# Attention and mixture of experts on one core: seven products from the fourth expert unit on, beside the last attention heads

## The chip, the cores and the metric

One core of a Trainium2 chip runs the whole program. The metric is the device time of one execution in microseconds (us); the times below are those of three runs, and the profile is one more execution with the hardware profiler on. PE is TensorE, DVE VectorE, ACT ScalarE, POOL GpSimd, SP SyncE, whose queue issues nearly all DMAs.

## The reference, cut to what matters

```python
# q, k, v: (2, 8, 768, 64); proj: (64, 6)
q_bucket, k_bucket = 6 sign bits of q @ proj and of k @ proj, as a number
scores = where(q_bucket == k_bucket, q @ k.T / 8, -1e9)
attn = softmax(scores); attn_out = attn @ v
x = attn_out as (2 * 768, 512)
# probs: (1536, 4), rows made to sum to 1; w1: (4, 512, 1024); w2: (4, 1024, 512)
for e in range(4):
    h = maximum(x @ w1[e], 0)
    out += p[:, e:e+1] * (h @ w2[e])
```

Everything is float32.

## The kernel before, in words

**Heads.** There are two batches of 8 heads, counted here as heads 0 to 15; heads 8 to 15 are batch 1. A head has 6 tiles of 128 rows of scores. `stage_s` ("S") makes a tile by 4 matmuls into the tile `sps` (two of them, taken in turn) from a head's four stacks `q1`, `al`, `ah`, `k2`, and a DVE instruction (line 432) takes the tile out and its row minimum. One step later ACT takes the exponential (448), two steps later DVE turns blocks (512, tile `t1`); after three tiles these go through DRAM (`scr`, `pt`). `stage_v` ("V") multiplies by `v` seven steps after the head's end, in 24 matmul records, and `stage_u` copies the result `pv` into `xraw`. `prep_head` makes the next head's stacks while a head runs: ACT writes `ah`; POOL copies it into `q1` (twice) and `k2`; DVE writes `al`; POOL copies `al` into `ah`; PE makes the hash `hps`; ACT writes its signs into `k2`; POOL turns them into bits in `al` and copies these into `k2`. The stacks have two buffers each, so a head's stacks are made while the head before still reads its own.

**Units.** A batch of the expert layer is 8 units (4 experts in two halves), 16 in all, counted 0 to 15. A unit has a first layer (x @ w1 into `hh` and `hl`, high and low halves of the ReLU) and a second layer (six tiles of 128 rows, each 12 matmuls of 512 columns into one PSUM bank `mps`, which DVE then adds to `acc`, line 754). All factors are split into a high and a low half, and a product is three matmuls. Units 0 to 5 (`unit`) make the first layer by 96 matmuls of 384 columns. Units 6 to 15 (`unit_fast`, from `FAST` on) make it by seven products of sums of blocks in place of eight, with 84 matmuls; their factors are sums of blocks of x (t1 to t4, by `x_ops_first` for batch 0, `x_ops_early` and `x_ops_late` for batch 1) and of w1 (s1 to s4, by `split_w1_fast` in the second layer of the unit before). In a sum, `combine` or `mix` is the DVE subtraction, then ACT writes the high half and POOL or DVE the low one. `mt` tiles hold the sums of products.

**Order.** Each engine runs its instructions in the order in which the program writes them. Attention of batch 1 is a generator, `attention()`, whose yields are costs; after each piece of an expert unit the main loop draws as much attention as a fixed pace allows:

```python
        while da < dm * ATT_PACE * n_att / n_moe:
            x = next(att, None)
```

Before, the attention is drawn to its end (`drained`) ahead of unit 5's second layer, and `x_ops_first` and the first call of `split_w1_fast` run in unit 5, when all scores have been made.

**PSUM.** Of eight banks, `ps2` holds two tiles of two banks each (`sps` during attention, `pa` and `pd` of a fast unit after it), and `ps1` four tiles of one bank (`mps`, `pv`, `hps`).

Of the kernel before, what the change touches and what calls it, by code (L numbers as in the profile page):

```python
# [48 lines left out]
FAST = 6  # L49
# [3 lines left out]
def tile_lsh_attention__then__domain_moe(  # L53
# [366 lines left out]
    def stage_s(b, h, t):  # L420
# [9 lines left out]
        pt = pp.tile([P, S], F32, tag="p", name="p")  # L430
# [179 lines left out]
    def attention():  # L610
# [3 lines left out]
        def do(op, i):  # L614
# [57 lines left out]
            elif op == "P":  # L672
                if i < n:
                    b, h, t = seq[i]
                    c = next(prep[0], None) if t >= PREP_AT else None
                    x = hseq.index((b, h))
                    if t == NT - 1 and x + 2 < len(hseq) and in_blocks(*hseq[x + 2]):
# [3 lines left out]
                    if t == NT - 1 and x + 1 < len(hseq):  # L681
                        load_v(*hseq[x + 1])
# [81 lines left out]
    def second_layer(b, u, first_u, hs, w2, xo=None):  # L764
# [6 lines left out]
        for s in range(NS - 1, -1, -1) if blocks else range(NS):  # L771
            for t in range(TS):
# [419 lines left out]
```

## Time and profile before

| what | value |
|---|---|
| median of three runs | 710.18 us (709.97 to 710.18) |
| the profiled execution: its own time | 710.34 us |
| its span, first to last instruction | 708.6 us |
| PE, DVE, ACT, POOL busy | 99%, 69%, 47%, 45% of the span |

The profiled execution is 0.16 us above the median, and 1.7 us of its time lie around the span. A matmul's record overlaps the next one's, so the rate of PE is read from starts, not from durations. In rows of groups, "mean ns" is the mean duration of one instruction; in a timeline the first number is the start and the second the duration, both in us from the span's start, and of a row "x2" the duration is that of both together.

### The profile page before, as it was taken

How to read it: one execution, taken by the hardware profiler on the slowest of the kernel's cores; microseconds unless marked ns; L12 is line 12 of the kernel's file. 1: busy time of each engine (PE TensorE's matmuls, PEld its weight loads, DVE VectorE, ACT ScalarE, POOL GpSimd, SP SyncE). 2: the span in 40 equal slices, each digit the busy share in tenths (PEclk: the TensorE clock that was granted, in tenths of full speed). 3: DMA queues.
4: the chain of work that ended last, by engine and by line, in shares of the span. 5: the costliest groups of instructions: out<-in, count | busy, mean ns of one | idle time of the engine just before them, and what ended most of it. 6: DMA issues, size and time to landing. Idle time of an engine off the chain costs nothing.

```text
span 708.6 us, 10175 instructions
## 1 busy us (share of the span) xinstructions
PE 700.9 (99%) x3726; PEld 593.9 (84%) x3726; DVE 490.2 (69%) x782; ACT 333.6 (47%) x655; POOL 316.5 (45%) x290
## 2 busy tenths in 40 slices
PE   8999999999999999999999999999999999999997
PEld 6766675878887978978888989899898989989896
DVE  6898888865585754755228797886857667685762
ACT  6887788543453544524234444343433434353340
POOL 6359578523352453503238555543514234341420
PEclk9999999999999999999999999999999999999999
DMA  6323354768997977867931121421212121122202
GB/s 150 68 47 75 75 116 84 216 170 204 264 247 225 238 182 223 238 214 231 237 105 60 61 89 54 153 63 60 93 57 90 46 75 59 61 90 59 90 1 89
DMA packets 90848, 87.76 MB, mean 124 GB/s; under 512 B 53168, under 2 KB 55728, under 8 KB 90800
## 3 DMA queue, kind: packets, MB, share of 16 engines
q1 hardware_dynamic: 89776, 86.80, 44.2%
q8 instruction: 29, 0.48, 0.3%
q10 hardware_dynamic: 1024, 0.33, 0.2%
q14 instruction: 19, 0.16, 0.1%
HBM read 65.04 MB, written 22.07 MB: 123 GB/s over the span
## 4 chain that ended last, share of the span: by engine, by line
PE 93%; DVE 2%; POOL 2%; issue 1%; ACT 1%; DMA 0%; POOLq 0%; DVEq 0%
PE mps L760 12%; PE mps L762 12%; PE mps L761 12%; PE pv L547 8%; PE mps L808 5%; PE mps L810 5%; PE mps L809 5%; PE sps L427 4%; PE sps L425 4%; PE ptps L493 4%; PE mps L1051 3%; PE mps L1050 3%; PE mps L1047 3%; PE pa L1050 2%; PE pa L1051 2%; PE pd L1051 2%
## 5 line engine op out<-in xcount | busy, mean ns | idle before, releaser
L760 PE MATMUL mps<-w2hi,hh 128*128 128x512 f32 (+1 forms) x388 | 151.0, 389 | 0.0
L761 PE MATMUL mps<-w2lo,hh 128*128 128x512 f32 (+1 forms) x388 | 150.5, 388 | 0.0
L762 PE MATMUL mps<-w2hi,hl 128*128 128x512 f32 (+1 forms) x388 | 150.4, 388 | 0.0
L1033 POOL TENSOR_TENSOR w2lo<-ws,w2hi 128x512 fp32r<-128x512 f32 x40 | 50.7, 1287 | 124.0 <-ACT w2hi L1032 121.1
L432 DVE TENSOR_SCALAR_CACHE_REDUCE p<-sps 128x768 f32<-128x768 f32 x96 | 90.0, 939 | 17.8 <-PE sps L427 16.3
L754 DVE SCALAR_TENSOR_TENSOR acc<-mps,pe,acc 128x512 f32<-128x512 f32 (+1 forms) x85 | 62.9, 740 | 56.0 <-PE mps L762 55.7
L448 ACT ACTIVATE p<-p,nb 128x768 f32<-128x768 f32 x96 | 89.5, 933 | 23.4 <-DVE p L432 23.0
L762 PEld LDWEIGHTS mps<-w2hi,hl 128*128 128x128 f32 x388 | 72.9, 188 | 15.7
L760 PEld LDWEIGHTS mps<-w2hi,hh 128*128 128x128 f32 x388 | 72.8, 188 | 15.0 <-issue 1.2
L761 PEld LDWEIGHTS mps<-w2lo,hh 128*128 128x128 f32 x388 | 72.9, 188 | 14.0
L547 PE MATMUL pv<-pt,tv 128*64 128x384 f32 x288 | 67.1, 492 | 0.0
L992 POOL TENSOR_TENSOR w1lo<-ws,w1hi 128x512 fp32r<-128x512 f32 x30 | 47.5, 1589 | 41.9 <-ACT w1hi L988 41.7
L808 PE MATMUL mps<-xs,w1hi 128*128 128x384 f32 x192 | 65.1, 339 | 0.0
L810 PE MATMUL mps<-xs,w1lo 128*128 128x384 f32 x192 | 64.5, 336 | 0.0
L809 PE MATMUL mps<-xs,w1hi 128*128 128x384 f32 x192 | 64.5, 336 | 0.0
L843 ACT ACTIVATE hh<-mps 128x384 fp32r<-128x384 f32 x48 | 23.4, 489 | 84.6 <-PE mps L810 84.6
L1060 ACT ACTIVATE hh<-mt 128x384 fp32r<-128x384 f32 x60 | 31.5, 525 | 58.4 <-DVE mt L1105 38.0
L844 DVE SCALAR_TENSOR_TENSOR hl<-mps,hh 128x384 fp32r<-128x384 f32 x48 | 26.4, 554 | 46.0 <-ACT hh L843 45.7
L425 PE MATMUL sps<-ah,q 128*128 128x384 f32 x192 | 53.5, 359 | 0.4 <-DVE p L432 0.4
L547 PEld LDWEIGHTS pv<-pt,tv 128*64 128x64 f32 x288 | 24.9, 136 | 32.2 <-issue 30.7
L512 DVE STREAM_TRANSPOSE t<-p 128x768 f32<-128x768 f32 x48 | 46.3, 965 | 7.7 <-ACT p L448 7.6
L242 POOL TENSOR_SCALAR q<-ah 64x768 fp32r<-64x768 f32 (+1 forms) x33 | 27.1, 821 | 54.5 <-ACT ah L354 40.1
(160 smaller groups left out, 1528.6 us busy)
## 6 DMA issues: line engine op xcount, KB each, us to landing
ws<-in_moe_w_dram SPq DMA_DIRECT2D x64, 512.0 KB, 3.9
scr<-t SPq DMA_DIRECT2D x16, 1152.0 KB, 7.5
pt<-scr SPq DMA_DIRECT2D x64, 288.0 KB, 5.7
tv<-in_v_dram SPq DMA_DIRECT2D x16, 192.0 KB, 4.5
tqk<-in_q_dram SPq DMA_DIRECT2D x30, 96.0 KB, 3.3
out_dram<-acc SPq DMA_DIRECT2D x11, 256.0 KB, 2.0
tqk<-in_k_dram SPq DMA_DIRECT2D x28, 96.0 KB, 3.1
rdb<-row SPq DMA_DIRECT2D x14, 192.0 KB, 6.4
```

The lines of the kernel that those rows point to most:

```text
L425: nc.tensor.matmul(ps[:, i, :NH], q1[:, sl], k1[:, i * NH : (i + 1) * NH], start=True, stop=False)
L432: nc.vector.tensor_scalar(out=two(pt), in0=ps[:, :, :NH], scalar1=MASKED, scalar2=MASKED, op0=ALU.min, op1=ALU.min, accum_out=nb,)
L448: nc.scalar.activation(pt, pt, ACTF.Exp, bias=nb, scale=-1.0, accum_out=dens[b, h, r][:, o : o + 1])
L547: nc.tensor.matmul(dst, vvs[b, h][:, c], pts[b, h, g][c], start=c == 0, stop=c == NT - 1, tile_position=(0, g * D),)
L754: nc.vector.scalar_tensor_tensor(out=acc, in0=ps, scalar=pcol, in1=acc, op0=ALU.mult, op1=ALU.add)
L760: nc.tensor.matmul(ps, hh[:, ts], w2hi[:, f, cs], start=n == 0, stop=False)
L761: nc.tensor.matmul(ps, hh[:, ts], w2lo[:, f, cs], start=False, stop=False)
L762: nc.tensor.matmul(ps, hl[:, ts], w2hi[:, f, cs], start=False, stop=n == FC - 1)
L808: nc.tensor.matmul(ps[:, :SB], w1hi[:, kk, fs], xhi[b, kk][:, sl], start=kk == 0, stop=False)
L809: nc.tensor.matmul(ps[:, :SB], w1hi[:, kk, fs], xlo[b, kk][:, sl], start=False, stop=False)
L810: nc.tensor.matmul(ps[:, :SB], w1lo[:, kk, fs], xhi[b, kk][:, sl], start=False, stop=kk == KD - 1)
L1033: nc.gpsimd.tensor_tensor(out=lo[:, c + o], in0=t[:, o], in1=hi[:, c + o].bitcast(F32), op=ALU.subtract)
```

## The change

`FAST` goes from 6 to 4, so units 4 and 5 use seven products too, while attention still runs beside unit 4. To make room:

- the sums of x for batch 0 are made in unit 3's first layer (t2, t3, t4) and at the start of its second layer (t1's halves, written over halves that unit 3 no longer reads);
- sums of both kinds and the products' `mt` tiles share a tag of their own, `pm`, with two buffers; the score tiles `p` of batch 1 have four in place of six, those of batch 0 alternate between both tags;
- a batch 0 fast unit keeps `pa` and `pd` in one-bank tiles, so that all its sums share `ps1` with `pv` and `hps`; its sums are made in place in the `mt` tiles, and it yields after each product;
- the stacks have one buffer per tag, in two sets for heads 0 to 13 by turns; heads 14 and 15 (`ALONE`) use the same set, so head 15's preparation is written after head 14's last tile of scores, followed by a yield of `ALONE_GAP`;
- `v` of a head is loaded in its own second step, from two buffers, in place of the last step of the head before, from three;
- the operands of batch 1 are spread over other tiles, six of seven in units 5 and 6.

```diff
-FAST = 6
+FAST = 4
+ALONE = 14
+ALONE_GAP = 2100
+EARLY = 5
...
+    def p_tile(b):
+        p_turn[0] += 1
+        if b == 0 and p_turn[0] % PP_BUFS >= PP_BUFS - 2:
+            return pair_tile([P, S], "p")
+        return pp.tile([P, S], F32, tag="p", name="p")
+
+    def pair_tile(shape, name):
+        return pp.tile(shape, F32, tag="pm", name=name, bufs=2)
...
     def stack_tiles(b, h):
-        heads[b, h] = tuple(stk.tile([P, S], F32R, tag=n, name=n) for n in ("q1", "al", "ah", "k2"))
+        x = b * H + h
+        side = "b" if x < ALONE and x % 2 else ""
+        heads[b, h] = tuple(stk.tile([P, S], F32R, tag=n + side, name=n) for n in ("q1", "al", "ah", "k2"))
...
-                    c = next(prep[0], None) if t >= PREP_AT else None
                     x = hseq.index((b, h))
-                    if t == NT - 1 and x + 2 < len(hseq) and in_blocks(*hseq[x + 2]):
+                    c = next(prep[0], None) if t >= PREP_AT and x < ALONE else None
+                    if t == NT - 1 and x + 2 < len(hseq) and in_blocks(*hseq[x + 2]) and x < ALONE:
                         turn_blocks(*hseq[x + 2])
...
-                    if t == NT - 1 and x + 1 < len(hseq):
-                        load_v(*hseq[x + 1])
+                    if t == 1 and x:
+                        load_v(*hseq[x])
...
+            x, t = divmod(i, NT)
+            if t == NT - 1 and ALONE <= x < len(hseq) - 1:
+                for c in prep[0]:
+                    yield c
+                if x + 2 < len(hseq):
+                    turn_blocks(*hseq[x + 2])
+                yield ALONE_GAP
...
-        if first_u + u + 1 == FAST:
-            drained()
-        xo = early if first_u + u + 1 == FAST else None
+        xo = x_ops_last() if first_u + u + 1 == FAST else None
...
+    def keep_halves(ops, name, raw):
+        for kk in range(KH):
+            h, l = (x[kk] for x in ops[name])
+            nc.scalar.activation(h, raw[:, kk], ACTF.Copy)
+            nc.gpsimd.tensor_tensor(out=l, in0=raw[:, kk], in1=h.bitcast(F32), op=ALU.subtract)
...
     def x_ops_first():
...
+        t1, t2 = (pair_tile([P, KH, SB], "xc") for _ in range(2))
+        nc.vector.tensor_tensor(out=t1, in0=b12, in1=b11, op=ALU.subtract)
+        nc.vector.tensor_tensor(out=t2, in0=b22, in1=t1, op=ALU.subtract)
+        yield
+        pair_in("t2", ((stk, "q1b"), (stk, "alb")))
+        keep(xop, "t2", t2)
+        nc.vector.tensor_tensor(out=b22, in0=b22, in1=b12, op=ALU.subtract)
+        yield
+        pair_in("t3", ((stk, "ahb"), (stk, "k2b")))
+        keep(xop, "t3", b22)
+        yield
+        nc.vector.tensor_tensor(out=t2, in0=t2, in1=b21, op=ALU.subtract)
+        pair_in("t4", ((xp, "xe0"),))
+        keep(xop, "t4", t2)
+        sums[0] = t1
+        yield
+
+    def x_ops_last():
+        xop["t1"] = in_halves()
+        keep_halves(xop, "t1", sums.pop(0))
+        yield
...
+        def mix(x, y, op, t=None):
+            if t is None:
+                t = pair_tile([P, KH, HF], "wc")
             nc.vector.tensor_tensor(out=t, in0=x, in1=y, op=op)
             return t
...
+        def acc(name, half):
+            return one("mps")[:, :SB] if b == 0 or half else big(name)[:, 0, :SB]
...
+        ma, mb = (pair_tile([P, 2, SB], "mt") for _ in range(2))
+        s1, u2, s5, u3 = ma[:, 0], ma[:, 1], mb[:, 0], mb[:, 1]
         for j in range(2):
...
             product(pd, w["s4"], xop["b22"], j, False)
-            c12 = tmp(ld, "tqk")
-            nc.vector.tensor_tensor(out=c12, in0=pd, in1=u2, op=ALU.add)
-            hidden_hi(1, j, c12)
+            nc.vector.tensor_tensor(out=s1, in0=pd, in1=u2, op=ALU.add)
+            hidden_hi(1, j, s1)
+            yield 1120
...
-        if not b:
-            xo = early if first_u + u + 1 < NU else x_ops_late()
+        if b == 0 and u >= EARLY:
+            drained()
+            xo = early if u + 1 < NU else x_ops_late()
```

The first place is the change from head 14 to head 15. On PE, the rows run from head 14's last tile of scores (`sps_3314` before, `sps_3310` now) to head 15's first (`sps_3343`, `sps_3412`); before, 12 matmuls of unit 3's second layer lie between them:

```order
L425 MATMUL sps_3314<-ah_2860,q1_2858 128x384 x2
L427 MATMUL sps_3314<-k2_2861,al_2859 128x384 x2
L760 MATMUL mps_3322<-w2hi_3048,hh_3044 128x512
L761 MATMUL mps_3322<-w2lo_3049,hh_3044 128x512
...
L425 MATMUL sps_3343<-ah_3122,q1_3120 128x384 x2
L427 MATMUL sps_3343<-k2_3123,al_3121 128x384 x2
```

Now there are 12 of that layer, the hash of head 15, and 36 more:

```order
L441 MATMUL sps_3310<-ah_2858,q1_2856 128x384 x2
L443 MATMUL sps_3310<-k2_2859,al_2857 128x384 x2
L783 MATMUL mps_3318<-w2hi_3048,hh_3044 128x512
...
L385 MATMUL hps_3346<-xt_3073,pf_109 44x384 x2
L783 MATMUL mps_3353<-w2hi_3048,hh_3044 128x512
...
L441 MATMUL sps_3412<-ah_3340,q1_3338 128x384 x2
L443 MATMUL sps_3412<-k2_3341,al_3339 128x384 x2
```

The hash, which stood in unit 3's first layer, has moved between the two heads. On POOL, head 15's preparation stood before between the low halves of unit 3's w2:

```order
L719 TENSOR_TENSOR w2lo_3049<-ws_2983,w2hi_3048 128x512 x2
L242 TENSOR_SCALAR q1_3120<-ah_3122 64x768 x2
L242 TENSOR_SCALAR k2_3123<-ah_3122 64x768
L719 TENSOR_TENSOR w2lo_3049<-ws_3029,w2hi_3048 128x512 x2
L242 TENSOR_SCALAR ah_3122<-al_3121 64x768
L384 TENSOR_SCALAR al_3121<-k2_3123,bit_mul_105 44x768
L242 TENSOR_SCALAR k2_3123<-al_3121 12x768
```

Now it stands behind the low half of t4 (`xo_3275`), that of a11, the two of t1 (`xs0`) and that of a12, with a22's inside it:

```order
L908 TENSOR_TENSOR xo_3275<-xc_3069,xo_3275 128x768
L1008 TENSOR_TENSOR w1lo_3293<-ws_3189,w1hi_3292 128x512
L917 TENSOR_TENSOR xs0_114<-xc_3068,xs0_114 128x384
L917 TENSOR_TENSOR xs0_115<-xc_3068,xs0_115 128x384
L1008 TENSOR_TENSOR w1lo_3293<-ws_3240,w1hi_3292 128x512
L258 TENSOR_SCALAR q1_3338<-ah_3340 64x768 x2
L258 TENSOR_SCALAR k2_3341<-ah_3340 64x768
L258 TENSOR_SCALAR ah_3340<-al_3339 64x768
L1008 TENSOR_TENSOR w1lo2_3295<-ws_3240,w1hi2_3294 128x512
L400 TENSOR_SCALAR al_3339<-k2_3341,bit_mul_105 44x768
L258 TENSOR_SCALAR k2_3341<-al_3339 12x768
```

Six instructions of the seven products' operands have come in among it. On DVE, before, head 14's last scores (`sps_3314`) are taken out between two additions to `acc`:

```order
L754 SCALAR_TENSOR_TENSOR acc_1998<-mps_3295,pe_113,acc_1998 128x512
L512 STREAM_TRANSPOSE t1_3312<-p_3258 128x6x4x32
L432 TENSOR_SCALAR p_3319,nb_3320<-sps_3314 128x768
L754 SCALAR_TENSOR_TENSOR acc_2049<-mps_3322,pe_113,acc_2049 128x512
L512 STREAM_TRANSPOSE t1_3312<-p_3292 128x6x4x32
```

Now, with what each row waits for in brackets, t4's sum (line 937) and the sums s1 and s2 of w1 (`wc`) stand ahead of them:

```order
L937 TENSOR_TENSOR xc_3069<-xc_3069,xr_120 128x768 [waits Pool_49]
L777 SCALAR_TENSOR_TENSOR acc_1966<-mps_3278,pe_113,acc_1966 128x512 [waits PE_49]
L1013 TENSOR_TENSOR wc_3296<-ws_3189,ws_3240 128x512 [waits DMAHW7_49,DMAHW1_49,Pool_49]
L1013 TENSOR_TENSOR wc_3300<-wc_3296,ws_3189 128x512 [waits DVE_49,Pool_49]
L528 STREAM_TRANSPOSE t1_3308<-p_3222 128x6x4x32 [waits DMAHW5_49,Activation_49]
L448 TENSOR_SCALAR p_3315,nb_3316<-sps_3310 128x768 [waits PE_49]
L777 SCALAR_TENSOR_TENSOR acc_1996<-mps_3318,pe_113,acc_1996 128x512 [waits PE_49]
L1008 TENSOR_TENSOR w1lo_3293<-wc_3296,w1hi_3292 128x512 [waits Activation_49]
L373 SCALAR_TENSOR_TENSOR al_3339<-xt_3073,qk_scale_103,ah_3340 128x768 [waits Activation_49]
```

`wc_3296` (s1) and `wc_3300` (s2) take the two buffers of `pm` that t2, from which t4 is made in place, and t1 hold, so s1 waits for POOL's row of `xo_3275` and s2 for its second row of `xs0`.

The second place is DVE in unit 4's first layer, from head 15's second tile of scores on; before, such a layer had between two score tiles only one or two `hl`:

```order
L512 STREAM_TRANSPOSE t1_3418<-p_3425 128x6x4x32
L432 TENSOR_SCALAR p_3494,nb_3495<-sps_3489 128x768
L844 SCALAR_TENSOR_TENSOR hl_3473<-mps_3497,hh_3472 128x384
L844 SCALAR_TENSOR_TENSOR hl_3473<-mps_3514,hh_3472 128x384
L512 STREAM_TRANSPOSE t1_3533<-p_3454 128x6x4x32
L432 TENSOR_SCALAR p_3540,nb_3541<-sps_3535 128x768
```

Now the products' sums stand between them:

```order
L528 STREAM_TRANSPOSE t1_3480<-p_3461 128x6x4x32
L448 TENSOR_SCALAR p_3518,nb_3519<-sps_3513 128x768
L1079 SCALAR_TENSOR_TENSOR hl_3528<-mps_3466,hh_3527 128x384
L1114 TENSOR_TENSOR mt_3464<-mps_3490,mt_3464 128x384
L1119 TENSOR_TENSOR mt_3465<-mps_3549,mt_3464 128x384
L1120 TENSOR_TENSOR mt_3465<-mt_3465 128x384
L1079 SCALAR_TENSOR_TENSOR hl_3547<-mt_3464,hh_3546 128x384
L1079 SCALAR_TENSOR_TENSOR hl_3547<-mt_3465,hh_3546 128x384
L528 STREAM_TRANSPOSE t1_3480<-p_3487 128x6x4x32
L448 TENSOR_SCALAR p_3576,nb_3577<-sps_3571 128x768
```

Five tiles of scores of head 15, ten sums (lines 1104 to 1128) and eight `hl` stand on DVE between the unit's first matmul and its last.

## Rows read from the trace of the kernel before

**Rows 1.** The page: span, PE's busy time, and the chain that ended last, by engine.
```profile
span 708.6 us, 10175 instructions
PE 700.9 (99%) x3726; PEld 593.9 (84%) x3726; DVE 490.2 (69%) x782; ACT 333.6 (47%) x655; POOL 316.5 (45%) x290
PE 93%; DVE 2%; POOL 2%; issue 1%; ACT 1%; DMA 0%; POOLq 0%; DVEq 0%
```

**Rows 2.** Windows: window, length, busy PE PEld DVE ACT POOL, granted clock, DMA.
```profile
160.00:330.00 170.00, 170.00 (x890) 144.12 (x890) 108.28 (x183) 75.43 (x149) 68.14 (x63) 1.00 0.85 232
```

**Rows 3.** PE's timeline in unit 3 and at both ends of unit 6's products.
```profile
287.96 0.34 PE L808 MATMUL mps<-xs,w1hi 128*128 128x384 f32 x1
...
292.16 0.51 PE L425 MATMUL sps<-ah,q 128*128 128x384 f32 x2
...
292.85 0.40 PE L760 MATMUL mps<-w2hi,hh 128*128 128x512 f32 x1
...
295.61 0.51 PE L425 MATMUL sps<-ah,q 128*128 128x384 f32 x2
...
393.86 0.33 PE L1047 MATMUL pa<-xs,w1hi 128*128 128x384 f32 x1
...
408.57 0.39 PE L760 MATMUL mps<-w2hi,hh 128*128 128x512 f32 x1
```

**Rows 4.** The chain that ended last, in order of time: V and the hash.
```profile
275.56 4.02 PE pv L547 x24
279.58 0.65 PE hps L369 x4
```

**Rows 5.** DMA issues of the page: KB, median us from issue to landing.
```profile
tv<-in_v_dram SPq DMA_DIRECT2D x16, 192.0 KB, 4.5
```

**Rows 6.** Timeline of all engines where unit 4's second layer begins.
```profile
340.24 0.39 PE L760 MATMUL mps<-w2hi,hh 128*128 128x512 f32 x1
...
340.44 0.49 ACT L843 ACTIVATE hh<-mps 128x384 fp32r<-128x384 f32 x1 [1.59 <-PE mps L810]
...
340.96 0.56 DVE L844 SCALAR_TENSOR_TENSOR hl<-mps,hh 128x384 fp32r<-128x384 f32 x1 [1.52 <-ACT hh L843]
```

**Rows 7.** DVE's timeline: score tiles, sums of x, s2, a sum of products.
```profile
296.48 0.97 DVE L512 STREAM_TRANSPOSE t<-p 128x768 f32<-128x768 f32 x1
297.37 0.92 DVE L432 TENSOR_SCALAR_CACHE_REDUCE p<-sps 128x768 f32<-128x768 f32 x1
...
374.53 1.64 DVE L879 TENSOR_TENSOR xc<-xc,xr 128x768 f32<-128x768 f32 x1
376.09 0.95 DVE L879 TENSOR_TENSOR xc<-xr 128x768 f32<-128x768 f32 x1
...
382.24 1.58 DVE L996 TENSOR_TENSOR wc<-wc,ws 128x512 f32<-128x512 f32 x1
...
400.97 1.37 DVE L1105 TENSOR_TENSOR mt<-mt 128x384 f32<-128x384 f32 x1
```

**Rows 8.** ACT's timeline: an exponential, head 15's `ah`, a high half of x.
```profile
277.66 0.92 ACT L448 ACTIVATE p<-p,nb 128x768 f32<-128x768 f32 x1
...
278.58 0.92 ACT L354 ACTIVATE ah<-xt,qk_scale 128x768 fp32r<-128x768 f32 x1
...
378.56 0.85 ACT L871 ACTIVATE xo<-xc 128x768 fp32r<-128x768 f32 x1
```

**Rows 9.** POOL's timeline: head 15's copies and bits, low halves of w1 and x.
```profile
279.59 1.73 POOL L242 TENSOR_SCALAR q<-ah 64x768 fp32r<-64x768 f32 x2 [4.43 <-ACT ah L354]
...
341.89 2.55 POOL L719 TENSOR_TENSOR w1lo<-ws,w1hi 128x512 fp32r<-128x512 f32 x2 [11.62 <-ACT w1hi L727]
...
378.00 3.66 POOL L875 TENSOR_TENSOR xo<-xc,xo 128x768 fp32r<-128x768 f32 x2 [2.64 <-ACT xo L871]
...
384.86 3.45 POOL L992 TENSOR_TENSOR w1lo<-ws,w1hi 128x512 fp32r<-128x512 f32 x2
```

**Rows 10.** Groups of POOL, by line and shape, 340 to 708 us: low halves of 384 columns.
```profile
L956 POOL TENSOR_TENSOR xs<-xraw,xs 128x384 fp32r<-128x384 f32 x2 | 2.0, 1012 | 0.0
```

More of the change, by code (lines that the diff above doesn't have):

```diff
@@ L429, in stage_s @@
             )
-        pt = pp.tile([P, S], F32, tag="p", name="p")
+        pt = p_tile(b)
         nb = sm.tile([P, 1], F32, tag="nb", name="nb")
@@ L795, in second_layer @@
                 next(sp, 0)
-                if xo is not None and (nxt == NU or tt % 2 and (blocks or tt < NT - 1)):
+                if xo is not None and (nxt == NU or tt % 2 or not blocks):
                     next(xo, 0)
@@ L889, in slices, with keep, in_halves @@
         xop[name] = tuple([x[0, j + kk][:, sl] for kk in range(KH)] for x in (xhi, xlo))
+    def keep(ops, name, raw):
+        h, l = ops[name]
+        nc.scalar.activation(h, raw, ACTF.Copy)
+        nc.gpsimd.tensor_tensor(out=l, in0=raw, in1=h.bitcast(F32), op=ALU.subtract)
+    def in_halves():
+        return tuple([x[0, kk][:, right] for kk in range(KH)] for x in (xhi, xlo))
+    def keep_halves(ops, name, raw):
[3 more added lines that the diff above has]
+            nc.gpsimd.tensor_tensor(out=l, in0=raw[:, kk], in1=h.bitcast(F32), op=ALU.subtract)
+    sums = {}
     def x_ops_first():
@@ L920, in x_ops_early, with pair @@
     def x_ops_early():
[L921 to L935 removed]
+        b11, b12, b21, b22 = x_blocks(1)
+        def pair(name, pool, *tags, **kw):
+            shape = [P, 2 // len(tags), KH, SB]
+            ts = [pool.tile(shape, F32R, tag=tag, name="xo", **kw) for tag in tags]
+            next_ops[name] = tuple(t[:, i] for t in ts for i in range(2 // len(tags)))
+        pair("b11", stk, "q1", "al")
+        keep(next_ops, "b11", b11)
         yield
[L937 removed]
+        pair("t1", stk, "ah", "k2")
         t1 = combine(b12, b11, ALU.subtract)
[L939 to L940 removed]
+        keep(next_ops, "t1", t1)
         yield
@@ L948, in x_ops_early @@
         t4 = combine(t2, b21, ALU.subtract)
-        hi("t4", t4)
-        lo("t4", t4, nc.gpsimd)
+        keep(next_ops, "t4", t4)
         yield
-        next_ops["b21"] = tuple([x[0, kk][:, right] for kk in range(KH)] for x in (xhi, xlo))
-        for kk in range(KH):
-            h, l = (x[kk] for x in next_ops["b21"])
-            nc.scalar.activation(h, b21[:, kk], ACTF.Copy)
-            nc.gpsimd.tensor_tensor(out=l, in0=b21[:, kk], in1=h.bitcast(F32), op=ALU.subtract)
+        pair("b21", ptp, "pt")
+        keep(next_ops, "b21", b21)
+        yield
+        pair("b22", ptp, "pt")
+        keep(next_ops, "b22", b22)
         yield
@@ L1004, in split_w1_fast @@
         yield
-        s3 = mix(a11, a21, ALU.subtract)
         his("s1", s1)
         los("a12", a12, nc.gpsimd)
-        s4 = mix(a12, s2, ALU.subtract)
+        los("s1", s1, nc.vector)
         his("s2", s2)
         yield
-        los("s1", s1, nc.vector)
+        los("s2", s2, nc.vector)
+        s3 = mix(a11, a21, ALU.subtract)
         his("a22", a22)
@@ L1086, in unit_fast @@
             if j:
-                hidden(0, 1 + j, c21)
-            pd = big("pd")[:, 0, :SB]
+                hidden(0, 1 + j, u3)
+            yield 1120
+            pd = acc("pd", 0)
             product(pd, w["s1"], xop["t1"], j, True)
             nc.scalar.activation(s5, pd, ACTF.Copy)
-            pb = one("mps")[:, :SB]
+            yield 1120
+            pb = acc("mps", 1)
             product(pb, w["s2"], xop["t2"], j, True)
             nc.vector.tensor_tensor(out=u2, in0=pb, in1=s1, op=ALU.add)
+            yield 1120
             product(pa, w["a12"], xop["b21"], j, False)
```

99 lines of the change are left out of this document (25 added, 74 removed).

## The prediction

> **What bounds the kernel now.** I read the page first. The reader is to see that PE is busy for 99% of a span of 708.6 us and makes up 93% of the chain that ended last [rows 1]. So time is won only by taking work from PE, and lost only by making PE wait. Next the window in which batch 1's scores run beside units 0 to 3: PE is busy for 170.00 of 170.00 us, DVE for 108, ACT for 75, POOL for 68, and the granted clock is 1.00 (the upper level, 2.4 GHz) [rows 2]. There is room on every other engine, on the average; a wait can come only from a chain of hand-overs that is longer than the PE work beside it. The third view is PE's timeline, for prices by starts: 24 matmuls of an ordinary first layer take 292.16 − 287.96 = 4.20 us (0.175 each), a tile of scores 292.85 − 292.16 = 0.69, 12 matmuls of a second layer 295.61 − 292.85 = 2.76, and unit 6's 84 product matmuls, with nothing beside them, 408.57 − 393.86 = 14.71 (0.175 each) [rows 3]. A head's V takes 4.02 and a hash 0.65 [rows 4].
>
> **What is taken away.** Units 4 and 5 have 96 first-layer matmuls each before and 84 after, 24 fewer at the same 0.175 us: **−4.2 us**. This stands on PE, which nothing covers, so it is the whole gain. That products run at full rate beside scores is taken from the equal step of both kinds; the order shows that they are really there.
>
> **What is moved at no price.** The new split of units 4 and 5 puts more on DVE, ACT and POOL, which have 36% to 60% of their time free [rows 2]. The loads of `v` are issued a step after the head begins in place of before it; they land 4.5 us after issue [rows 5], and at least eight tiles of scores (8 × 0.69 = 5.5 us, without the expert work between them) lie ahead of their V. If that cover failed, a V would be late by 4.5 us at the most; I take 0. The batch 1 operands, drawn early and late, stand beside second layers of 16.6 us (72 matmuls at 0.23), in which PE needs nothing from them; without that cover each pair would cost a POOL row of 1.83 [rows 9]. The sums in place add no instruction. All these I put at 0.
>
> **The first wait: head 15's first scores.** Its stacks may be written only after head 14's last tile of scores, since both use one set. That tile stands after 12 matmuls of unit 3's second layer. I count from the first matmul of that layer. PE reaches head 15's last two matmuls (the ones that need the bits in `k2`) after 2.76 + 0.69 + 2.76 + 0.65 + 3 × 2.76 + 0.35 = **15.5 us**.
>
> The other side of it starts at the same point, because PE's last `mps` of the first layer comes at its end. ACT writes `hh` 0.20 after the first matmul, and DVE's `hl` ends at 1.28 (340.96 + 0.56 − 340.24) [rows 6]. Then, in the order shown in the section on the change:
> - DVE makes t4. That takes 0.95 with POOL still and 1.64 beside it [rows 7]; POOL is still here, so it ends at 2.25.
> - ACT's high half of t4 takes 0.85 [rows 8], to 3.1; POOL's low half 1.83 (two in 3.66) [rows 9], to 4.95.
> - POOL's a11 takes between 1.28 (two in 2.55) and 1.73 (two in 3.45) [rows 9]; I take 1.5, the middle, since DVE's s1 runs over part of it: 6.45. The two halves of t1 take 1.01 each [rows 10]: 8.5.
> - s2 on DVE waits for t1's buffer, so it starts only now, and takes 1.58, as the like sum did beside POOL [rows 7]: 10.1. ACT's high half of s2 has 512 columns, and an `hh` of 384 takes 0.49 [rows 6], so some 0.6: 10.7.
> - ACT then has head 14's exponential ahead of head 15's `ah`, 0.92 each [rows 8]: 12.55.
> - POOL's three copies and the one of `al` take 0.87 each (two in 1.73) [rows 9]: 16.0. a22's low half stands ahead of the bits: 1.5, 17.5. The bits and the last copy: 2 × 0.87, 19.25.
> - Some ten hand-overs at 0.03 (340.44 + 0.49 to 340.96) [rows 6] add 0.3: **19.6 us**.
>
> So PE waits 19.6 − 15.5 = **4.1 us**. What is queued behind is the whole of PE, since it runs in order: the last head's scores and unit 4. Bounds: with a11 and a22 at 1.28 (−0.44) and no time for hand-overs (−0.3) it is 3.4; with both at 1.73 (+0.46) and t4's sum beside POOL at 1.64 (+0.69) it is 5.3.
>
> One rule bears on s2. [rows 7, 9] show a sum of two SBUF inputs at 1.58 beside a POOL pair at 3.45: both are longer than alone (POOL 1.28 each), and neither is held for the whole of the other. The Trainium skill, "SBUF — State Buffer", section "Who interferes with whom", says that such a sum and a GpSimd instruction that reads SBUF exclude each other for a whole instruction. By it s2 would start only after a12's low half, some 0.7 us later, the wait would be 4.8 and the sum below +2.5. The sum does not go by it.
>
> **The second wait: unit 4's last product.** In its first layer DVE must serve scores and sums by turns. From the end of head 15's second tile of scores until the sum that frees the bank of the last product, PE has 13 products of 1.05 (six matmuls) and four tiles of scores of 0.69: **16.4 us** of work [rows 3]. In that stretch DVE has, by the order, five takings-out of scores (0.92), four turnings of blocks (0.97, 0.89 from start to start), one sum on SBUF alone (1.37) [rows 7], and five sums with PSUM, four `hl` and one copy of `pv`, all at 0.56 like an `hl` [rows 6], with 0.35 for what is small: 4.6 + 3.6 + 1.4 + 5.6 + 0.35 = 15.5. DVE also stands still where an `hl` waits for its `hh` or a sum for ACT's copy: some five times, 0.5 to 0.6 each by the `hh` row [rows 6], 2.8. That makes 18.3, and a wait of **1.9 us**. Bounds: 0, if those waits of DVE fall where it would be idle anyway, and 3.2, if four sums cost a wait of half a microsecond more. Such a tight turn does not exist in the trace before, so this is the term that I trust least.
>
> Unit 5, which has no scores beside it but only the last head's V, has DVE nearly to itself, as unit 6 has now; unit 6 shows 84 matmuls without a gap [rows 3]. I put it at 0.
>
> **The sum.** −4.2 + 4.1 + 1.9 = **+1.8 us**, from −0.8 (3.4 and 0) to +4.3 (5.3 and 3.2). The profiled execution took 710.34 us, 0.16 above the median of 710.18. 710.34 + 1.8 = **712.1 us**. A measurement of this kernel can tell about 0.2%, 1.42 us, from no change: slower begins at 711.6, faster at 708.8.
>
> **The rivals.**
> - *Only the first wait.* DVE keeps pace in unit 4, because it has caught up while PE stood still. For it: DVE has 36% of its time idle in the stretch shown [rows 2]. Against it: 15.5 us of work in 16.4 leaves under 1 us for all of its waits. −4.2 + 4.1 gives 710.3, with the bounds 709.5 to 711.4: no change.
> - *Both waits hidden.* The chain of head 15's stacks need not take each price in full: if POOL makes t1's halves and t4 early, or DVE's sums of t4, s1 and s2 run into free engines, its last copy ends by 15.5 and PE never stops. The point that decides is that copy: of the 4.1 us, 2.7 must go, with no second wait, before the change is faster by 0.2%. Against it: POOL's part alone, from t4's low half to the last copy, is 1.83 + 1.5 + 2.0 + 4 × 0.87 + 1.5 + 1.74 = 12.1 us, and s2, its high half, the exponential and `ah` (4 us) lie within it, so 16 us after a start at 3.1 are missed only if a row is wrong by a lot. Time: 706.1 (nothing waits) to 708.7.
> - *The clock falls.* In the stretch shown PE never stops, and the granted clock is 1.00 [rows 2]; the change puts a stop of some 4 us into it. If the clock came down to its lower level (1.2 GHz), each microsecond of PE's work until it rises would take two. With 2.8 us of work (four tiles of scores) at that level the time is 714.9, with one half of unit 4's products (7.35) 719.5. No stop of that length is in these rows, so they speak neither for it nor against it, and I chose the two lengths. The Trainium skill, "TensorE: Matmul & The Clock Gate", says that an array that has stood idle goes back to 1.2 GHz. No run here shows it.
> - That the change doesn't do what it says is excluded: in the new order units 4 and 5 have 84 product matmuls each.
>
> **How the numbers follow.** Both waits as worked out: 0.50. Only the first: 0.24. Both hidden, or nearly: 0.17. The clock: 0.09. The likeliest gives **712.1 us**, with 709.5 to 714.6 as its own range; the 8 in 10 reach to 707.5 on the side of the hidden waits and to 715.0 on the other, and leave out the better half of the hidden case and most of the fall of the clock. Slower than 711.6: 0.33 of the first case, 0.06 of the second (a small second wait on top) and the clock's 0.09, 0.48. Within 0.2%: 0.16 of the first and 0.16 of the second, 0.32. Faster: 0.17 of the hidden case, 0.02 of the second and 0.01 of the first, 0.20.
>
> **What would show it.** Right: in the new trace PE's idle time by releaser has one gap of 3.4 to 5.3 us before head 15's first scores, released by POOL's copies into `ah` and `k2`, with s2 on DVE released by POOL; and one of up to 3 us at the last product of unit 4, released by DVE. The 84 product matmuls of units 4 and 5 at 0.175 each. Wrong: PE busy all through that stretch (then the chain's prices are too high, and the time is near 706); or long waits in places that I priced at 0, above all V waiting for `v`, unit 5's first products, or the batch 1 operands; or a granted clock below 1.00 behind the gap.

## The result, and the profile after

The changed kernel takes 720.45 us (median of 4, 719.53 to 722.16), the kernel before 710.15: a ratio of 1.0148, 95% interval 1.0128 to 1.0169. It is slower by 10.3 us, and lies above the range, which ended at 715.0. The profiled execution took 719.53 us with a span of 717.6 us, 9.0 us more than the 708.6 of before. The page of the changed kernel, where [rows 1] stood before:

```profile
PE 701.0 (98%) x3702; PEld 590.1 (82%) x3702; DVE 517.1 (72%) x816; ACT 342.7 (48%) x669; POOL 315.8 (44%) x290
PE   8999999999999999979899999999999999999998
PEclk9999999999999999979999999999999999999999
PE 84%; DVE 5%; POOL 5%; issue 3%; ACT 2%; DMA 1%; POOLq 0%; DVEq 0%; ACTq 0%
```

24 matmul records are gone, as the change says, yet PE is busy for as long as before. The 18th slice (about 305 to 323 us) shows both why there are gaps and why the busy time did not shrink: PE stands still in it, and its granted clock is lower. The waits of PE after the start, with us in total, times, and the longest:

```profile
PE sps L443 <- POOL k L258: 3.3, 2, 2.9
PE mps L1064 <- ACT mt L1103: 2.4, 1, 2.4
PE sps L441 <- POOL ah L258: 2.3, 1, 2.3
PE mps L785 <- DVE hl L1079: 1.8, 1, 1.8
```

Before, PE was busy for all of the stretch from 160 to 330 us [rows 2]. PE's timeline of the changed kernel at head 15's first scores:

```profile
308.19 0.39 PE L785 MATMUL mps<-w2hi,hl 128*128 128x512 f32 x1
310.84 1.01 PE L441 MATMUL sps<-ah,q 128*128 128x384 f32 x2 [2.27 <-POOL ah L258]
314.79 1.01 PE L443 MATMUL sps<-k,al 76*128 76x384 f32 x2 [2.94 <-POOL k L258]
315.59 0.63 PE L783 MATMUL mps<-w2hi,hh 128*128 128x512 f32 x1
...
320.85 2.53 PE L563 MATMUL pv<-pt,tv 128*64 128x384 f32 x14
```

Its windows there (window, length, PE busy, granted clock, DMA share and GB/s):

```profile
306.00:308.00 2.00, 2.00 (x11) 1.00 0.00 0
310.00:312.00 2.00, 1.01 (x2) 0.69 0.19 57
318.00:320.00 2.00, 2.00 (x6) 0.50 0.00 0
322.00:324.00 2.00, 2.00 (x16) 1.00 0.00 0
```

At full rate the scores would have started at 308.42 (308.19 + 0.23) and their second pair at 308.77; it started at 314.79, **6.0 us** late. The clock had fallen by the end of the first of the two stops (0.69 is the mean of 310 to 312 us), and was back at 1.00 by 322. From the second pair on, from 314.79 to 320.85, PE did a pair of scores (0.35) and 12 matmuls (2.76) in 6.06 us: the 12 step by 0.43 us at a granted clock of 0.50 (1.2 GHz) in place of 0.23 at 1.00 (2.4 GHz), **3.0 us** lost. A stop of 2.6 us in unit 4 (339.98 + 0.17 to 342.76) and one of 1.9 in unit 5's second layer follow. −4.2 + 6.0 + 3.0 + 2.6 + 1.9 = 9.3, against 9.0 in the spans.

What made the stacks late, from the timeline of the other engines. Unit 3's second layer begins at 292.66:

```profile
297.59 1.30 POOL L1008 TENSOR_TENSOR w1lo<-ws,w1hi 128x512 fp32r<-128x512 f32 x1
297.67 1.77 DVE L1013 TENSOR_TENSOR wc<-ws 128x512 f32<-128x512 f32 x1 [1.29 <-POOL xo L908]
298.84 2.46 POOL L917 TENSOR_TENSOR xs<-xc,xs 128x384 fp32r<-128x384 f32 x2
301.34 1.76 DVE L1013 TENSOR_TENSOR wc<-wc,ws 128x512 f32<-128x512 f32 x1 [1.90 <-POOL xs L917]
304.59 0.92 ACT L370 ACTIVATE ah<-xt,qk_scale 128x768 fp32r<-128x768 f32 x1
305.60 2.70 POOL L258 TENSOR_SCALAR q<-ah 64x768 fp32r<-64x768 f32 x2 [3.05 <-ACT ah L370]
306.03 1.58 DVE L373 SCALAR_TENSOR_TENSOR al<-xt,qk_scale,ah 128x768 fp32r<-128x768 f32 x1
308.38 1.18 POOL L258 TENSOR_SCALAR k<-ah 64x768 fp32r<-64x768 f32 x1
309.53 1.26 POOL L258 TENSOR_SCALAR ah<-al 64x768 fp32r<-64x768 f32 x1
310.68 0.68 DVE L1013 TENSOR_TENSOR wc<-ws,wc 128x512 f32<-128x512 f32 x1
310.87 1.62 POOL L1008 TENSOR_TENSOR w1lo<-ws,w1hi 128x512 fp32r<-128x512 f32 x1
312.60 1.22 POOL L400 TENSOR_SCALAR al<-k,bit_mul 44x768 fp32r<-44x768 f32 x1
313.90 0.83 POOL L258 TENSOR_SCALAR k<-al 12x768 fp32r<-12x768 f32 x1
```

The chain is the one that was worked out, link by link, and it is 22.1 us long (292.66 to 314.73), not 19.6. PE's own side took 16.1 (292.66 to 308.77) in place of 15.5, so the wait is 22.1 − 16.1 = 6.0. Until `ah` the chain keeps to the forecast: `ah` ends at 12.85 where 12.55 was said. Then come the four copies, 5.1 us in place of 3.5, and a22 and the bits, 2.84 in place of 2.4. The reason shows when a DVE sum that stood alone is put beside one that did not. In the kernel before, POOL is idle from 413.72 to 416.82, and in that time stands

```profile
414.30 0.69 DVE L996 TENSOR_TENSOR wc<-wc,ws 128x512 f32<-128x512 f32 x1
```

A sum of the same size takes 1.77 beside POOL's a11 (297.67 above). It ends at 299.44, 0.55 us after a11, which is most of its lone duration: it was held until POOL had finished, and the two POOL instructions behind it (L917) took 2.46 in place of 2 × 1.01 [rows 10]. It is the rule of the Trainium skill, "SBUF — State Buffer", section "Who interferes with whom", and the trace agrees: 1.77 against 0.69.

### The profile page after: what moved, and what is told of

Its sections match the earlier page's. It is cut to its first block, busy times and chain, and to the rows that moved or that the text cites. A ratio compares the mean times of both kernels' runs of the same rounds, so it can differ in the third digit from the quotient of the medians.

```text
span 717.6 us, 10186 instructions
## 1 busy us (share of the span) xinstructions
PE 701.0 (98%) x3702; PEld 590.1 (82%) x3702; DVE 517.1 (72%) x816; ACT 342.7 (48%) x669; POOL 315.8 (44%) x290
## 4 chain that ended last, share of the span: by engine, by line
PE 84%; DVE 5%; POOL 5%; issue 3%; ACT 2%; DMA 1%; POOLq 0%; DVEq 0%; ACTq 0%
PE mps L783 11%; PE mps L785 11%; PE mps L784 11%; PE pv L563 8%; PE mps L1064 4%; PE mps L1068 4%; PE mps L1067 4%; PE sps L443 4%; PE ptps L509 4%; PE sps L441 3%; PE mps L831 3%; PE mps L833 3%; PE mps L832 3%; PE pa L1064 2%; PE pd L1064 2%
## 5 line engine op out<-in xcount | busy, mean ns | idle before, releaser
L1050 POOL TENSOR_TENSOR w2lo<-ws,w2hi 128x512 fp32r<-128x512 f32 x48 | 61.3, 1300 | 152.0 <-ACT w2hi L1049 141.3
L1008 POOL TENSOR_TENSOR w1lo<-ws,w1hi 128x512 fp32r<-128x512 f32 x36 | 52.1, 1453 | 53.4 <-issue 41.4
L1074 ACT ACTIVATE hh<-mt 128x384 fp32r<-128x384 f32 x72 | 37.8, 525 | 72.7 <-DVE mt L1120 43.8
L1004 ACT ACTIVATE w1hi<-wc 128x512 fp32r<-128x512 f32 x48 | 30.1, 631 | 66.5 <-DVE wc L1013 66.4
L1079 DVE SCALAR_TENSOR_TENSOR hl<-mt,hh 128x384 fp32r<-128x384 f32 x72 | 42.8, 596 | 16.3 <-ACT hh L1074 13.6
L443 PE MATMUL sps<-k,al 76*128 76x384 f32 x192 | 50.3, 342 | 3.7 <-POOL k L258 3.3
L1068 PE MATMUL mps<-xo,w1lo 128*128 128x384 f32 x144 | 48.5, 337 | 0.0
L1067 PE MATMUL mps<-xo,w1hi 128*128 128x384 f32 x144 | 48.4, 336 | 0.0
```

The lines of the kernel that those rows point to most:

```text
L443: nc.tensor.matmul(ps[:, i, :NH], q2[0:MQE, sl], k2[0:MQE, i * NH : (i + 1) * NH], start=False, stop=True)
L1050: nc.gpsimd.tensor_tensor(out=lo[:, c + o], in0=t[:, o], in1=hi[:, c + o].bitcast(F32), op=ALU.subtract)
L1067: nc.tensor.matmul(ps, whi[:, kk, fs], xl[kk], start=False, stop=False, skip_group_check=True)
L1068: nc.tensor.matmul(ps, wlo[:, kk, fs], xh[kk], start=False, stop=kk == KH - 1, skip_group_check=True)
```

## The experiments

The ratios are to runs of the kernel before on the same chip, with their 95% intervals; that kernel took 710.49 to 710.78 us there, against 710.15 beside the changed kernel, which was not run again. So a difference from its 720.45 is one between chips, and those of runs 1, 3 and 5 (1.2 to 1.6 us) are not clear of noise: their intervals overlap its 1.0128 to 1.0169. Where a trace is quoted, it is that of the profiled execution.

**1. Work in place of the stop.** In `stage_s`, ahead of head 15's first scores:

```diff
+        if (b, h, t) == (B - 1, H - 1, 0):
+            for n in range(34):
+                nc.tensor.matmul(ps[:, 0, :SB], xhi[0, 3][:, SB : SB + P], xhi[0, 2][:, 0:SB], start=True, stop=True)
```

> The changed kernel with 34 more matmuls of 384 columns (5.95 us at 0.175 each) ahead of head 15's first scores, into the same PSUM tile, which the scores then overwrite. Theory A (the stop of PE itself lowers its clock): PE works where it waited, the granted clock stays at 1.00, the scores start no later, and the 12 second-layer matmuls behind them go at 0.23 again, not 0.43: 3.0 to 3.5 us less than the changed kernel's 720.45, so about 717.2. Theory B (the slow matmuls come from something else, such as the DMA or the other engines busy there): they stay slow, and the time stays within 1 us of 720.45.

718.91 us, 1.0122 (1.0106 to 1.0137), 1.5 us less than the changed kernel. The added matmuls fill the stop, the granted clock is 1.00 through it, and neither wait for the stacks is left. But this time the clock fell behind the second stop, which is as long as in the changed kernel's profile, where it did not (1.00 from 343 us on):

```profile
312.00:314.00 2.00, 2.00 (x13) 1.00 0.67 245
338.00:340.00 2.00, 0.00 (x0) 1.00 0.93 204
342.00:344.00 2.00, 2.00 (x8) 0.50 1.03 378
```

So theory A holds for the first stop by the trace: it is the stop that lowers the clock, since with PE at work and the DMAs there as before (0.67 against 0.65 of their time) it stays. In time the run fell short of the 3.0 to 3.5 us that theory A gave, since the clock fell behind the second stop. A stop of 2.4 us lowers it in some executions and not in others.

**2. The split of w1 two tiles later.** In `second_layer`:

```diff
-                next(sp, 0)
+                if nxt != FAST or tt >= 2:
+                    next(sp, 0)
```

> The changed kernel, with the first split of w1 for the seven products begun two tiles of 128 rows later, so that the sums s1 and s2 and the low halves of a11 and a12 stand behind head 15's stacks on DVE and POOL and not ahead of them. Theory A (the six operands' instructions on POOL and DVE make the stacks late): PE's wait of 6 us and the slow matmuls behind it go, about 9 us less than 720.45, so 711 to 712. Theory B (the wait is the single set of stacks alone, and the split has little to do with it): the wait stays above 3 us, the clock still falls, and the time stays above 716. Theory C: the wait moves to unit 4's first products, which then wait for the operands: up to 5 us of the 9 come back, 714 to 716.

713.67 us, 1.0037 (1.0024 to 1.0051), 6.8 us less. Head 15's scores follow at once (308.11 to 308.34). POOL's copies in its trace:

```profile
299.83 2.32 POOL L258 TENSOR_SCALAR q<-ah 64x768 fp32r<-64x768 f32 x2
300.15 1.30 DVE L373 SCALAR_TENSOR_TENSOR al<-xt,qk_scale,ah 128x768 fp32r<-128x768 f32 x1
302.23 0.83 POOL L258 TENSOR_SCALAR k<-ah 64x768 fp32r<-64x768 f32 x1
303.02 0.83 POOL L258 TENSOR_SCALAR ah<-al 64x768 fp32r<-64x768 f32 x1
304.55 1.60 DVE L1014 TENSOR_TENSOR wc<-wc,ws 128x512 f32<-128x512 f32 x1
305.71 1.23 POOL L400 TENSOR_SCALAR al<-k,bit_mul 44x768 fp32r<-44x768 f32 x1
```

The copies take 0.83 without a DVE sum beside them and 1.16 with one, the bits 1.23 with one. Theory A holds: the six operands ahead of the stacks were the first wait. The time is above theory A's 711 to 712, since the stops in units 4 and 5 (2.5 and 1.8 us) are still there, and in the profiled execution the clock fell behind each of them:

```profile
336.00:338.00 2.00, 2.00 (x7) 0.50 1.03 372
384.00:386.00 2.00, 2.00 (x6) 0.52 0.00 0
```

By PE's starts each fall costs 1.5 to 1.6 us: 13 steps from 334.43 to 338.25 take 3.82 in place of 2.28, and 10 from 382.19 to 386.07 take 3.88 in place of 2.30. Of the five executions one took 711.23 us at a mean clock of 0.999, and four 713.47 to 714.03 at 0.994 or 0.995, 2.2 to 2.8 us more, which is near the two falls together.

**3. All multiplications of batch 1's `xraw` on DVE.** In `stage_m`:

```diff
-        nc.gpsimd.tensor_tensor(out=x3, in0=x3, in1=rdb, op=ALU.mult)
+        (nc.vector if b else nc.gpsimd).tensor_tensor(out=x3, in0=x3, in1=rdb, op=ALU.mult)
```

> The changed kernel, with batch 1's multiplication of xraw by rdb (two per pair of heads, 128x384) on DVE in place of POOL. Theory A (DVE's hl from SBUF take 1.5 us in place of 0.6 because POOL's multiplication reads SBUF beside them, and this makes both the wait of 2.4 us in unit 4 and that of 1.8 us in unit 5): both waits shrink, 2 to 4 us less than 720.45, 716.5 to 718.5. Theory B (DVE simply has too much to do there): two more instructions on DVE lengthen them, 720.5 to 722.

719.29 us, 1.0124 (1.011 to 1.0138). The second stop of the changed kernel, in the timeline of all its engines:

```profile
335.19 3.04 POOL L601 TENSOR_TENSOR xraw<-xraw,rdb 128x384 f32<-128x384 f32 x2
335.57 3.08 DVE L1079 SCALAR_TENSOR_TENSOR hl<-mt,hh 128x384 fp32r<-128x384 f32 x2
340.31 0.54 DVE L1127 TENSOR_TENSOR mt<-mt,mps 128x384 f32<-128x384 f32 x1
340.89 0.52 ACT L1074 ACTIVATE hh<-mt 128x384 fp32r<-128x384 f32 x1 [3.18 <-DVE mt L1127]
342.24 0.47 ACT L1103 ACTIVATE mt<-mps 128x384 f32<-128x384 f32 x1
342.76 0.44 PE L1064 MATMUL mps<-xs,w1hi 128*128 128x384 f32 x1 [2.43 <-ACT mt L1103]
```

The same two `hl` in this run, and its new stop:

```profile
336.89 1.23 DVE L1079 SCALAR_TENSOR_TENSOR hl<-mt,hh 128x384 fp32r<-128x384 f32 x2
408.34 0.44 PE L1064 MATMUL mps<-xs,w1hi 128*128 128x384 f32 x1 [1.56 <-ACT mt L1097]
```

Without POOL beside them the two `hl` take 1.23, not 3.08; so far theory A holds. The stop in unit 4 shrinks only to 1.4, since DVE now has the multiplication itself (0.92 at 338.04, right behind them), that of unit 5 goes, and a new one of 1.6 us comes in unit 6. The time lies between the two theories' ranges. I read the stops as one lateness of DVE and POOL that shows where PE next needs them; this run alone does not show it.

**4. A longer gap.** `ALONE_GAP = 6000` in place of 2100.

> The changed kernel with ALONE_GAP 6000 in place of 2100: 66 matmuls (48 of the second layer, 18 of unit 4's first products) in place of 36 stand between head 15's hash and its first scores, 5.9 us more of PE's work. Theory A (the chain of the stacks has a fixed length of some 22 us from the start of unit 3's second layer): the wait of 6 us is covered but for a rest under 1 us, the clock does not fall, 9 us less: 711 to 712.5. Theory B (the chain is itself driven by PE's pace, or products ahead of the scores wait instead): the wait moves, and the time stays above 715.

714.38 us, 1.0049 (1.0036 to 1.0062). Both theories had a part: the first wait goes, but head 15 comes later, and then a V waits 3.2 us for turned blocks that have not yet come back from DRAM:

```profile
PE pv L563 <- DMA pt<-scr: 3.2, 1, 3.2
PE mps L1064 <- ACT mt L1097: 1.3, 1, 1.3
```

The 1.3 us are at unit 4's first products, which now stand ahead of the scores. Two more things show. The stops in unit 4's second half and in unit 5's second layer are gone: POOL's multiplications lie elsewhere now (335.87 and 343.74), and the two `hl` of unit 4 take 1.23. And behind the stop of 3.2 us (374.11 to 377.28), longer than any of the changed kernel's, the granted clock stays at 1.00:

```profile
378.00:380.00 2.00, 2.00 (x16) 1.00 0.18 42
```

**5 and 6. ACT's copy ahead of the high half**, alone and with the late split. In `unit_fast`:

```diff
-            if j:
-                hidden(0, 1 + j, u3)
             yield 1120
             pd = acc("pd", 0)
             product(pd, w["s1"], xop["t1"], j, True)
             nc.scalar.activation(s5, pd, ACTF.Copy)
+            if j:
+                hidden(0, 1 + j, u3)
```

> The changed kernel with one line moved: in the second half of a unit, ACT writes the high half of the first half's last sum behind its copy of the second product and not ahead of it. Theory A (PE's stop of 2.4 us in unit 4 is PE waiting to add to a bank that ACT has not yet copied, because ACT itself waits for a DVE sum): the stop shrinks by the high half (0.5 us) and by what that waits for, but the copy still stands behind an exponential that waits for DVE's scores, so some 1 to 1.5 us remain: 719 to 719.5. Theory B (the exponential had long been free): the stop goes, 717.5 to 718. Theory C (the stop has another cause): no change from 720.45.

> The split of w1 two tiles later, as before, and the line moved as in the run before this one. If a stop of PE of 2.8 us is what lets the clock fall in four of five executions of the split alone, a stop of half that length lets it fall in none: the time is 710 in all executions, with a granted clock of 1.00 throughout. If the clock falls for another reason, the times stay spread between 710 and 714.

718.83 us, 1.0128 (1.0114 to 1.0143), and 712.82, 1.0033 (1.002 to 1.0046). A miss: the stop in unit 4 is 2.2 us in both, now for a DVE sum (line 1107 in run 5, 1108 in 6) rather than for ACT, so what a stop of half the length does to the clock was not tested. Times and clocks of the second stay spread (711.34 at 1.000 to 714.83 at 0.995). ACT's order was only the last link; DVE was late itself.

**7 to 10. One stop after another.** Each is the one before it with one more edit: 7, the last pair's multiplication on DVE (on top of 6); 8, heads 12 and 13's multiplication two steps later (`+ 2 *` where the diff has `- 2 *`); 9, two steps earlier in place of later; 10, head 14's V one step later.

```diff
-        nc.gpsimd.tensor_tensor(out=x3, in0=x3, in1=rdb, op=ALU.mult)
+        (nc.vector if (b, h) == (B - 1, H - 1) else nc.gpsimd).tensor_tensor(out=x3, in0=x3, in1=rdb, op=ALU.mult)
...
-                        if h % 2 and lag == (u_lag(b, h) if (b, h) == (0, H - 1) else LAG_M[b] + g):
+                        if h % 2 and lag == (u_lag(b, h) if (b, h) == (0, H - 1) else LAG_M[b] + g - 2 * ((b, h) == (B - 1, H - 3))):
...
     def v_lags(b, h):
+        if (b, h) == (B - 1, H - 2):
+            return (8,)
```

> The run before this one, with the last pair of heads' multiplication of xraw by rdb on DVE in place of POOL. Theory A (PE's stop of 1.8 us at unit 5's second layer comes from POOL's multiplication, which makes a sum and two hl on DVE take 1.0 to 1.5 us each): the stop goes, 1.5 to 1.8 us less than the run before, 708 to 708.5, faster than the kernel before the change. Theory B: unit 6's first products then wait, as they did in the run with all multiplications on DVE, and nothing is gained.

> The run before this one, with the multiplication of heads 12 and 13 on POOL two steps later, behind all low halves of unit 4's w2. Theory A (DVE's two hl of 1.5 us each, beside that multiplication, are what makes DVE late in unit 4): they take 0.6 each, PE's stop there goes, and the time is 706.5 to 707.5. Theory B (the delay only moves to the sums of the unit's second half): another stop of 1 to 2 us there, and no gain.

> The run with the late split, the moved line and the last pair's multiplication on DVE, and now POOL's multiplication for heads 12 and 13 two steps earlier, where DVE takes out and turns scores and has no sum of two SBUF inputs. Theory A (it is that multiplication beside DVE's two hl from SBUF that makes DVE late in unit 4): the two hl take 0.6 each, PE's stop of 2.2 us at unit 4's second half goes. Theory B: they stay at 1.5, beside something else. In both cases head 14's V may then be reached before its turned blocks have landed, a stop of up to 3 us, and unit 6's stop of 2.4 us stays: 711 to 714.

> The run before this one, with head 14's V one step later, behind two tiles of unit 4's second layer. The stop for the turned blocks goes, and one of about 2.4 us at unit 6's first products is all that is left: 709.5 without a fall of the clock behind it, 712 with one.

713.45 us (1.0044, 1.0032 to 1.0056), 712.86 (1.004, 1.0026 to 1.0055), 713.51 (1.0037, 1.0024 to 1.0049) and 711.06 (1.0007, 0.9998 to 1.0017). In 7 unit 5's stop went and one of 2.4 us in unit 6 came: theory B. In 8 the two `hl` take 1.23 and the stop in unit 4 went, and PE then reached head 14's V 3.0 us before its blocks: no gain, as theory B said, for another reason. Behind these 3.0 us the granted clock is 1.00; the executions without a trace run up to 716.21 us. In 9 POOL's two multiplications lie beside takings-out and turnings, and nothing there is longer:

```profile
319.68 2.42 POOL L601 TENSOR_TENSOR xraw<-xraw,rdb 128x384 f32<-128x384 f32 x2 [5.31 <-ACT xraw L590]
320.69 0.98 DVE L528 STREAM_TRANSPOSE t<-p 128x768 f32<-128x768 f32 x1 [0.50 <-ACT p L464]
321.70 0.96 DVE L448 TENSOR_SCALAR_CACHE_REDUCE p<-sps 128x768 f32<-128x768 f32 x1
327.11 1.23 DVE L1080 SCALAR_TENSOR_TENSOR hl<-mt,hh 128x384 fp32r<-128x384 f32 x2
```

The stop in unit 4 is gone there (theory A), V's of 2.7 and unit 6's of 2.4 us are left. 10 removes V's. Its executions run from 709.14 to 712.76, about the 709.5 and 712 that were expected; the profiled one is the fastest, with 1.6 us of unit 6's stop left and no fall of the clock behind it. The mean clock does not explain all of the scatter: one execution took 710.28 at 0.997, another 711.06 at 1.000.

**11 and 12. Fewer operands per second layer, and other engines for two low halves.**

```diff
-                if xo is not None and (nxt == NU or tt % 2 or not blocks):
+                if xo is not None and (nxt == NU or (tt % 2 and tt != 1) or not blocks):
...
-            xo = early if u + 1 < NU else x_ops_late()
+            xo = early if u + 1 < NU else both(early, x_ops_late())
```

`both` draws one generator after the other. In 12, on top, `los("s1", ...)` goes to POOL and `los("s3", ...)` to DVE.

> The run before this one, with batch 1's operands drawn two in each of the second layers of units 5, 6 and 7 in place of three in units 5 and 6. Theory A (unit 5's second layer has more work for DVE's two-input sums and POOL's low halves, which do not overlap, than PE has matmuls, so unit 6's first copy by ACT is late): unit 6's stop goes as well, no stop over 1 us is left, the clock does not fall, and the time is 706.5 to 707.5 in all executions, 0.4% to 0.5% faster than the kernel before the change. Theory B: the stop moves to unit 7 or 8, 709 to 711.

> The run with two operands per second layer, with the low half of s1 on POOL and that of s3 on DVE, the other way round than before. Theory A (what is left of the stops at the first products of units 6, 7 and 8 is ACT's first copy, which writes the buffer that s3 held and waits for POOL's low half of s3): the buffer comes free a microsecond or two earlier, the rest of these stops goes, 1 to 1.5 us less than the run before: 708.8 to 709.5, faster than the kernel before the change by about 0.2%. Theory B (DVE's low half ends no earlier, since sums with two SBUF inputs wait for POOL anyway): no change from 710.3.

710.32 us, 0.9996 (0.9987 to 1.0005): no stop over 0.9 us is left behind the start, and the clock is 0.999 or 1.000 in each of the eleven executions. It is some 10 us faster than the changed kernel and equal to the one before. Of theory A the stops and the clock came true and the time did not: 706.5 to 707.5 was expected. 12 is a miss, 711.13, 1.0009 (1.0 to 1.0018). Its profiled execution is the slowest of its eleven (713.61), so its stops are no measure of the others; unit 7's first stop there is 1.8 us, released by DVE. DVE's low half of s3 ends 3.2 us after unit 7's first matmul (430.01 − 426.78), POOL's in 11 3.3 after it (427.99 − 424.72): no earlier, which is theory B.

## Why the prediction was wrong

The spans differ by 9.0 us where +1.8 was forecast. The terms as measured give 9.3, 7.5 too many: 3.0 from the fall of the clock, which stood outside the sum, 1.9 from the first wait, 1.9 from unit 5, which stood at 0, and 0.7 from the second wait.

- **What is taken away** was right: 24 records fewer, and units 6 to 15 have their products at the same rate. Unit 5's first layer fell from 20.89 us (356.60 to 377.49) to 18.89 (366.58 to 385.47) between PE's starts, 2.0 of the 2.1 us that 12 matmuls are.
- **The first wait** was the right place, chain and sign, and the size was off: 6.0 us, not 4.1, above the upper bound of 5.3. The term that failed is "POOL's three copies and the one of `al` take 0.87 each". It was read in a row of before with nothing of DVE beside it [rows 9]; here `al`, two low halves and the sum of s3 stand on DVE beside the copies, and they took 1.18 to 1.35 each, 1.7 us more in all; a22 and the bits add 0.5. Run 2 shows it: 0.83 without a DVE sum beside them. The kernel before had the price: four copies of earlier heads take up to 1.42 beside `al`.
- **The rule on s2** was set aside on a wrong reading. The sum of [rows 7] at 382.24 had ended before the pair of 3.45 began at 384.86 [rows 9]; beside it stood POOL's multiplication:

```profile
381.62 3.28 POOL L585 TENSOR_TENSOR xraw<-xraw,rdb 128x384 f32<-128x384 f32 x2
```

The sentence ahead of the rule, that "neither is held for the whole of the other", was not shown by these rows, and it took no lone price of DVE's sum, though the trace of before has one (0.69 at 414.30, shown in the section on the result): against it the 1.58 of [rows 7] is just such a hold. For s2 alone this mattered little (it ended at 10.4, not 10.1); it mattered for the copies, on which the rule was not tried.
- **The second wait** was near in size by luck, 2.4 to 2.6 for 1.9, within its bounds. That DVE is late in unit 4 was right; why was not. The prediction added up many short waits of DVE; the trace has two `hl` that read SBUF and cost 3.08 beside POOL's multiplication, where two at 0.56 were reckoned. In runs 4, 8 and 9, where they take 1.23, no stop is left in unit 4's second half, so the lateness of 1.9 that was worked out does not show once that cost is gone. The place was another too: not the last product's bank, but the fifth product of the second half, which adds to a bank that ACT must first copy.
- **Unit 5 at 0** failed: its second layer waited 1.9 us for an `hl`. "DVE nearly to itself, as unit 6 has now" overlooked POOL's multiplication of the last pair, which now falls there (386.13 to 388.80); beside and behind it stand

```profile
387.67 2.01 DVE L1079 SCALAR_TENSOR_TENSOR hl<-mt,hh 128x384 fp32r<-128x384 f32 x2
```

With that multiplication on DVE (run 7) the stop goes.
- **The clock** was named as a rival at 0.09, and it is the largest single part of the miss: 3.0 us in the profiled execution. Run 1 shows that the stop causes this fall. The gain and the three waits alone, −4.2 + 6.0 + 2.6 + 1.9, would give 6.3 us, still above the range's upper end. The two executions without a trace at 720.93 and 722.16 have a lower mean clock (0.990) than the two at 719.53 and 719.97 (0.992 and 0.995), so they may hold one more fall; where is not known. A fall need not be the change's: in the profiled executions of runs 3 and 7 one stands at 12 to 15 us, in code that all these kernels share.
- **A slip in the hidden case**: it says that 2.7 of the 4.1 us must go before the change is faster by 0.2%. By its own numbers 2.7 may stay (710.34 − 4.2 + 2.7 = 708.8) and 1.4 must go.
- **Where the gain of 4.2 us went** once the stops are taken away (run 11): between the start of unit 3's first layer and of unit 6's PE needed 125.47 us before and 124.34 there, 1.1 less. The other 3.1 us are slow steps and stops below 0.9 us, about half of them in the last head's V (5.56 in place of 4.02, 0.7 of it for turned blocks). The first layers of units 6 to 8 take 1.4 us more than before (45.5 against 44.1), and those of units 9 to 15 0.12 less each, which nobody forecast and no run explains. That the losses come from DVE and POOL holding each other up in the second layers is argued from their durations; run 12, which should have moved one of them, did not separate it.

## What to carry to other kernels

Price an instruction that reads SBUF by what stands beside it on the other of DVE and POOL, read its lone price only where the other engine is idle, and add the durations up on one line when both read: an average of free time on each engine did not show these waits. A wait of PE of some 2 us costs itself and, in some executions, slow steps behind it (1.5 to 3.0 us here), so put a fall of the clock into the price of such a stop, with a chance, and not only among the rivals. When removing a stop shows the next one of the same size, look for what all of them wait for before moving another instruction.

## What the runs showed of the hardware

- In the changed kernel the clock fell to 0.50 behind a stop of 2.3 us; after a second stop of 2.9 PE still worked at 0.50 for 6 us (steps of 0.43 in place of 0.23 us), and the clock was 1.00 again at 322 us. The length of a stop does not tell whether it falls: it fell behind stops of 2.4 (run 1), 2.5 and 1.8 us (run 2), and stayed at 1.00 behind 2.4 (the changed kernel's in unit 4), 3.0 (run 8) and 3.2 us (run 4).
- DVE's sum of two SBUF inputs of 128x512 takes 0.69 us alone and 1.77 beside POOL's a11; an `hl` from SBUF 0.56, and two of them 3.08 beside POOL's multiplication; POOL's copy of 64x768 0.83, and 1.35 beside DVE's `al`. Sums with one input from PSUM (0.55), takings-out (0.92 to 0.95) and turnings (0.97) were longer beside POOL by 0.03 at the most, by their medians.
